# Weight sums by another engine in another half of block 6, and tails loaded at other units, in a retention and gelu kernel

**Chip, cores, metric.** One core of a Trainium2 chip. The metric is the device time of one execution in microseconds. The time is 1.6 to 1.9 us longer than the span that a trace covers.

## The reference, cut

```python
def _attn_ref(q, k, v):                     # 8 batches, 8 heads, 576 positions, 64 wide
    scores = scale * np.matmul(q, k.transpose(0, 1, 3, 2))
    Dmat = np.where(rel >= 0, gamma[:, None, None] ** rel[None, :, :], 0.0)
    return np.matmul(scores * Dmat[None], v)

def _moe_ref(x, w_in, w_out):               # x: 4608 x 512, hidden 2048
    h = x @ w_in
    g = 0.5 * h * (1.0 + np.tanh(c * (h + 0.044715 * h * h * h)))
    return g @ w_out
```

The output of the first is the input of the second. All inputs and the output are float32; the kernel computes in float16 with float32 sums.

## The kernel before

The kernel walks through nine blocks t = 0 to 8 of 512 rows: up-projection, gelu, down-projection. Between the matmuls of block t it prepares the retention of a later batch. All of it is one program with a hand-set order: `at(t, u, f)` puts f behind step ("unit") u of block t. That sets the **order on each engine's queue**, not a time. 576 = 4 x 128 + 64: the last 64 positions of a batch are its "tail", loaded by GpSimd's DMA queue, cast to float16 by GpSimd (k, q) and ScalarE (v), and turned by a DMA transpose.

The down-projection needs seven products in place of eight, of sums of the activations (`act_sums`, VectorE, in each block) and sums of the weights. Blocks 7 and 8 do the up-projection in the same way, so sums of `w_in` are needed from block 7 on (`in_sums`, the "first weights").

```python
    def in_sums(names, eng):                        # L464: 128 x 1024 float16
        for o in names:
            wu[o] = ring16().rearrange("p (k n) -> p k n", k=2)
            ...
            eng.tensor_tensor(out=wu[o], in0=x, in1=y, op=f)

    def act_sums(t, f0, f1, us=slice(0, 2), part=(0, 1)):   # four times a block, 128 x 512 float16
        ...
            nc.vector.tensor_tensor(out=s["1"], in0=a21, in1=a22, op=ALU.add)        # L588
            nc.vector.tensor_tensor(out=s["2"], in0=s["1"], in1=a11, op=ALU.subtract)  # L589
        ...
        nc.vector.tensor_tensor(out=a21, in0=a11, in1=a21, op=ALU.subtract)          # L592
        nc.vector.tensor_tensor(out=s["4"], in0=a12, in1=s["2"], op=ALU.subtract)    # L593
    ...
    TAILS = {b: ((b + 2, 5), (b + 2, 14), (b + 2, 14)) for b in range(5)}   # load; cast k, q; cast v
    TAILS |= {5: ((6, 15), (6, 24), (6, 24)), 6: ((6, 25), (7, 4), (7, 4)), 7: ((7, 5), (7, 13), (7, 13))}
    ...
    for n, o in enumerate("1324"):
        at(6, 3 + 2 * n, lambda o=o: in_sums(o, P))        # P: GpSimd
```

The product opB (L610, "m = 6") takes s2, of which the fourth group of sums writes the last part.

## Time and profile before

| | before |
|---|---|
| median of the first three runs | 302.74 us (302.4 to 303.84) |
| the execution that the profile shows | 304.62 us, span 302.8, mean clock 0.993 |
| block 6 in that profile | 35.04 us |
| blocks 3 to 5 | 30.4 to 30.5 us |

The lines of the profile stand in the prediction. There, an L number is a line of the kernel; DVE is VectorE, POOL GpSimd, ACT ScalarE, PE TensorE; a line of a timeline has start, duration, engine, line, operation, output and input, and in brackets how long the engine had been idle and whom it waited for.

### The profile page before, as it was taken

Reading aid. Unit: us, or ns where it says so; the run is one execution under the profiler, and the core shown is the slowest. Engines: PE = TensorE matmul, PEld = TensorE weight load, DVE = VectorE, ACT = ScalarE, POOL = GpSimd, SP = SyncE. Lnnn points to the kernel's source line nnn. Section 1 sums busy time; section 2 is a strip of 40 time slices with the busy share of each in tenths; the row PEclk is TensorE's granted clock in tenths of the full one; section 3 lists DMA queues with packets and bytes.
Section 4 is the critical chain, followed back from the end, with each engine's and each line's share of the span. In section 5 each row is a group of like instructions: output and inputs, shape, how many; then the busy total and the mean of one; then the engine's idle time right before and its main releaser. Section 6 shows DMA issues by size and latency. Waiting matters only on the chain.

```text
span 302.8 us, 7015 instructions
## 1 busy us (share of the span) xinstructions
PE 291.4 (96%) x2795; PEld 203.4 (67%) x2795; DVE 196.3 (65%) x387; ACT 173.4 (57%) x336; POOL 129.3 (43%) x182
## 2 busy tenths in 40 slices
PE   6999999999999999999999999999995999999994
PEld 3568755788874587458745874588454876786683
DVE  7651889578963765476448653865598457947844
ACT  6666417998666574667466746673655047513820
POOL 8678215550925079107810681069999000000000
PEclk9999999999999999999999999999999899999999
DMA  7999999999999996999699979916722032003004
GB/s 202 216 340 365 386 282 222 215 247 229 219 202 225 185 258 140 217 207 249 115 215 214 223 104 224 277 23 99 235 72 78 28 122 72 0 2 141 0 3 139
DMA packets 130433, 52.90 MB, mean 175 GB/s; under 512 B 118752, under 2 KB 121056, under 8 KB 130400
## 3 DMA queue, kind: packets, MB, share of 16 engines
q1 hardware_dynamic: 128464, 48.77, 72.9%
q0 software_dynamic: 1536, 3.15, 3.9%
q8 instruction: 22, 0.36, 0.6%
q10 hardware_dynamic: 400, 0.52, 0.5%
q14 instruction: 11, 0.09, 0.1%
HBM read 36.70 MB, written 9.44 MB: 152 GB/s over the span
## 4 chain that ended last, share of the span: by engine, by line
PE 83%; DVE 5%; SPq 4%; ACT 3%; DMA 2%; issue 1%; POOL 0%
PE hp L416 24%; PE opB L610 14%; PE opC L610 10%; PE opA L610 9%; PE hp L433 8%; PE op L550 4%; SPq L95 3%; PE st L318 3%; PE xs L368 2%; PE xs L389 2%; DMA ld<-in_moe_w_in_dram 2%; PE hB L499 2%; PE us L339 2%; DVE s L589 1%; PE hC L499 1%
## 5 line engine op out<-in xcount | busy, mean ns | idle before, releaser
L416 PE MATMUL hp<-xT,w_in_sb 128*128 128x512 f16 x384 | 88.0, 379 | 0.1
L422 ACT ACTIVATE gT<-hp 128x512 f16<-128x512 f32 x96 | 57.4, 598 | 45.7 <-PE hp L416 45.2
L416 PEld LDWEIGHTS <-w_in_sb 128*128 128x128 f16 x384 | 36.8, 98 | 41.5 <-issue 2.3
L610 PEld LDWEIGHTS <-gT 128*128 128x128 f16 x512 | 50.0, 98 | 7.3
L325 DVE TENSOR_TENSOR ret<-st,cm 128x512 f16<-128x512 f32 x64 | 40.0, 681 | 10.2 <-PE st L318 10.2
L610 PEld LDWEIGHTS <-s 128*128 128x128 f16 x384 | 37.0, 99 | 8.8 <-DVE s L589 3.4
L258 POOL TENSOR_TENSOR ck<-ld,sc 128x512 f16<-128x512 f32 x31 | 32.7, 1055 | 22.1 <-DMA ld<-in_k_dram 22.1
L588 DVE TENSOR_TENSOR s<-gT 128x512 f16<-128x512 f16 x32 | 15.8, 493 | 28.5 <-ACT gT L422 26.9
L610 PE MATMUL opA<-w_out_sb,gT 128*128 128x256 f16 x256 | 30.6, 273 | 0.0
L610 PE MATMUL opB<-wt,gT 128*128 128x256 f16 x256 | 30.4, 273 | 0.0
L433 PE MATMUL hp<-xT,w_in_sb 128*128 128x256 f16 x256 | 29.8, 273 | 0.5 <-POOL w_in_sb L685 0.4
L861 POOL COPY gate<-s 128x1 f16<-128x1 f16 x5 | 0.9, 189 | 62.7 <-DVE s L593 62.7
L433 PEld LDWEIGHTS <-w_in_sb 128*128 128x128 f16 x256 | 24.6, 98 | 3.9 <-POOL w_in_sb L685 0.7
L258 POOL TENSOR_TENSOR cq<-ld,sc 128x512 f16<-128x512 f32 x24 | 25.8, 1076 | 2.0 <-DMA ld<-in_q_dram 1.8
L662 ACT COPY ost<-opA 128x512 f32<-128x512 f32 x8 | 4.7, 586 | 31.9 <-PE opA L610 28.6
L439 ACT ACTIVATE gT<-hp 128x512 f16<-128x512 f32 x32 | 19.0, 600 | 5.9 <-PE hp L433 5.8
L406 ACT CAST xT<-xs 128x512 f16<-128x512 f32 x32 | 18.4, 585 | 3.1 <-PE xs L389 2.7
L625 DVE TENSOR_TENSOR ost<-k,opC 128x512 f32<-128x512 f32 x15 | 10.3, 687 | 15.2 <-PE opC L610 14.9
L360 ACT CAST tbd<-ws 64x256 f16<-64x256 f32 x48 | 19.3, 403 | 1.4 <-DVE ws L355 0.8
L625 DVE TENSOR_TENSOR k<-k,opB 128x512 f32<-128x512 f32 (+1 forms) x18 | 11.2, 627 | 12.1 <-PE opB L610 10.6
L610 PE MATMUL opB<-wt,s 128*128 128x256 f16 x128 | 15.5, 273 | 3.1 <-DVE s L589 3.1
L589 DVE TENSOR_TENSOR s<-s,gT 128x512 f16<-128x512 f16 x32 | 16.1, 504 | 1.1
(126 smaller groups left out, 437.9 us busy)
## 6 DMA issues: line engine op xcount, KB each, us to landing
ld<-in_q_dram SPq DMA_DIRECT2D x32, 256.0 KB, 5.1
ld<-in_k_dram SPq DMA_DIRECT2D x32, 256.0 KB, 5.2
ld<-in_v_dram SPq DMA_DIRECT2D x32, 256.0 KB, 5.0
out_dram<-ost SPq DMA_DIRECT2D x16, 512.0 KB, 5.2
ld<-in_moe_w_in_dram SPq DMA_DIRECT2D x16, 256.0 KB, 5.5
ld<-in_moe_w_out_dram SPq DMA_DIRECT2D x16, 256.0 KB, 5.7
lt<-in_k_dram POOLq DMA_DIRECT2D x16, 64.0 KB, 4.5
lt<-in_q_dram POOLq DMA_DIRECT2D x16, 64.0 KB, 4.1
```

The costliest lines, as they stand in the source:

```text
L258: eng.tensor_tensor(out=dst.rearrange("p (h d) -> p h d", d=D), in0=raw.rearrange("p (h d) -> p h d", d=D), in1=sc[:, s0 : s0 + nh].unsque ...
L325: nc.vector.tensor_tensor(out=r, in0=st[hl][:, 0:w], in1=m.rearrange("p n i -> p (n i)"), op=ALU.mult)
L360: cp(out=(tbd[b % 2][r, c, :, r] if c < NC - 1 else tbt[b % 4][r, :, r]), in_=att[b]["w", c][r])
L406: nc.scalar.copy(out=xT[:, g0 : g0 + 2], in_=src)
L416: nc.tensor.matmul(hp.rearrange("p (g t) -> p g t", t=TL), w_in_sb[:, ct, 128 * fc : 128 * fc + 128], xT[:, o : o + TB // TL, ct, :], star ...
L422: nc.scalar.activation(out=gT[t][:, fc].rearrange("p i n -> p (i n)"), in_=hp, func=AF.Gelu_apprx_tanh)
L433: nc.tensor.matmul(hp[:, 256 * x : 256 * x + 256].rearrange("p (g t) -> p g t", t=TL), w_in_sb[:, ct, 128 * (f + x) : 128 * (f + x) + 128] ...
L439: nc.scalar.activation(out=gT[t][:, f : f + 2, 2 * u : 2 * u + 2, :].rearrange("p f i n -> p f (i n)"), in_=hp.rearrange("p (f n) -> p f n ...
L588: nc.vector.tensor_tensor(out=s["1"], in0=a21, in1=a22, op=ALU.add)
L589: nc.vector.tensor_tensor(out=s["2"], in0=s["1"], in1=a11, op=ALU.subtract)
L610: nc.tensor.matmul(op[tag, u][:, HD * u : HD * u + HD], lhs(f), rhs[:, f], start=(new and (u == 0 or own) and f == 0), stop=(f == NH - 1), ...
L625: nc.vector.tensor_tensor(out=o, in0=a, in1=b, op=ALU.add)
```

## The change

Intent: take the weight sums of w_in from GpSimd, where they run beside VectorE's activation sums, and give them to VectorE in the second half of block 6, where it has idle spells of 2.54 and 3.21 us in the trace of before. The tails of batches 4 to 7 are set to other units, so that their casts fit the new order.

```diff
     TAILS[0] = ((2, 5), (2, 20), (2, 20))
-    TAILS |= {5: ((6, 15), (6, 24), (6, 24)), 6: ((6, 25), (7, 4), (7, 4)), 7: ((7, 5), (7, 13), (7, 13))}
+    TAILS |= {4: ((6, 2), (6, 12), (6, 12)), 5: ((6, 18), (6, 26), (6, 26))}
+    TAILS |= {6: ((6, 27), (7, 5), (7, 5)), 7: ((7, 6), (7, 13), (7, 13))}
@@
     for n, o in enumerate("1324"):
-        at(6, 3 + 2 * n, lambda o=o: in_sums(o, P))
+        at(6, (22, 24, 26, 28)[n], lambda o=o: in_sums(o, V))
```

## The prediction

> **What bounds the kernel now.** I read the page first: which engine is busy, and which chain ended last.
>
> ```profile
> PE 291.4 (96%) x2795; PEld 203.4 (67%) x2795; DVE 196.3 (65%) x387; ACT 173.4 (57%) x336; POOL 129.3 (43%) x182
> ...
> PEclk9999999999999999999999999999999899999999
> ...
> PE 83%; DVE 5%; SPq 4%; ACT 3%; DMA 2%; issue 1%; POOL 0%
> ```
>
> TensorE (PE) is busy 96% of the span and carries 83% of the chain. Two things stand out: 5% of the chain lies on VectorE (DVE), and one slice of forty, near 235 us, has a lower clock. So I took the busy times of each engine by block. A block starts where the first up-projection matmul (L416) follows the last opB product of the block before: 89.3, 119.5, 149.9, 180.3, 210.8 for blocks 2 to 6, and 245.8 for block 7.
>
> ```profile
> core 0: us, PE busy (x) PEld busy (x) DVE busy (x) ACT busy (x) POOL busy (x), PEclk, DMA share, GB/s
> ...
> 149.90:180.30 30.40, 30.38 (x297) 20.25 (x296) 17.88 (x38) 18.42 (x36) 12.93 (x18) 1.00 0.97 184
> 180.30:210.80 30.50, 30.48 (x298) 20.24 (x296) 17.87 (x38) 18.42 (x36) 13.05 (x15) 1.00 0.83 165
> 210.80:245.80 35.00, 31.87 (x282) 20.80 (x281) 23.55 (x35) 15.59 (x30) 24.21 (x32) 0.95 0.34 93
> ```
>
> Blocks 3 to 5 take 30.4 to 30.5 us with PE never idle. Block 6 takes 35.0 us, though it has 16 matmuls fewer (no state products for a further block). GpSimd (POOL) is busy 24.2 us there instead of 13, and VectorE 23.6 instead of 17.9 with three instructions fewer: they take longer each. The loss sits in that block alone. Where it falls, the timelines of VectorE and GpSimd over the first half of block 6 say:
>
> ```profile
> 215.14 0.84 DVE L588 TENSOR_TENSOR s<-gT 128x512 f16<-128x512 f16 x1 [3.62 <-ACT gT L422]
> 216.01 2.22 DVE L589 TENSOR_TENSOR s<-s,gT 128x512 f16<-128x512 f16 x1
> 218.16 2.34 DVE L592 TENSOR_TENSOR gT<-gT 128x512 f16<-128x512 f16 x1
> 220.42 0.83 DVE L593 TENSOR_TENSOR s<-gT,s 128x512 f16<-128x512 f16 x1
> 221.17 2.47 DVE L325 TENSOR_TENSOR ret<-st,cm 128x512 f16<-128x512 f32 x4
> ...
> 230.57 1.40 DVE L588 TENSOR_TENSOR s<-gT 128x512 f16<-128x512 f16 x1
> 232.01 0.42 DVE L589 TENSOR_TENSOR s<-s,gT 128x512 f16<-128x512 f16 x1
> ```
> ```profile
> 213.55 2.14 POOL L464 TENSOR_TENSOR ld<-w_in_sb 128x1024 f16<-128x1024 f16 x1
> 215.77 2.19 POOL L464 TENSOR_TENSOR ld<-ld,w_in_sb 128x1024 f16<-128x1024 f16 x1
> 218.03 2.19 POOL L464 TENSOR_TENSOR ld<-w_in_sb,ld 128x1024 f16<-128x1024 f16 x1
> ```
>
> In block 5 the same four activation sums (L588 to L593) take 0.42 us each (184.69 to 186.2). Here two take 2.22 and 2.34, each ending within 0.3 us of the GpSimd weight sum (L464) beside it. L325, which reads one operand from PSUM, keeps its 0.62 each.
>
> ```profile
> 228.56 0.82 PE L610 MATMUL opB<-wt,s 128*128 128x256 f16 x6
> 232.49 1.29 PE L610 MATMUL opB<-wt,s 128*128 128x256 f16 x10 [3.11 <-DVE s L589]
> ...
> 234.68 3.04 PE L610 MATMUL opC<-wt,s 128*128 128x256 f16 x16
> ```
>
> PE gets six products into opB and waits 3.11 us for the last sum s2. Afterwards opC's sixteen products take 3.04 us instead of 1.9; the stretches 232.5 to 234.7 and 234.7 to 237.7 show a granted clock of 0.75 and 0.62. The loss is thus 3.11 us of waiting plus the slow clock behind it.
>
> [...] 2.22 against 0.42 us for the sums, no change for L325. [...] Here a gap of 3.11 us is followed by 0.62 to 0.75 for about 5 us. [...] The eight weight sums of w_out (L576), of the same 128x1024 f16 size as L464[...]: 0.68 us where nothing disturbs them, against 2.2 us on GpSimd.
>
> **The change, part by part.**
> (1) *Removed from GpSimd:* four L464, 2.31 + 2.14 + 2.19 + 2.19 = 8.8 us, of which the last three meet VectorE's sums. VectorE's excess against 0.42 each is 0.42 + 1.80 + 1.92 + 0.41 = 4.55 us up to 221.2; the last 0.41 belongs to the cast of tail 4, which begins at 220.18. Later casts of tails 5 and 6 (at 225.4 and 230.4) add 0.86 + 0.41 + 0.43 + 0.98 = 2.7 us. Together 7.2 us. Block 5 has slack for 1.59 + 2.11 = 3.7 us (its idle times before L325 and before the fourth L588). 7.2 − 3.7 = 3.5, close to the 3.11 us for which PE waited and the 0.3 us by which block 5's last s2 comes early. This closes, so the cause is settled for me.
> (2) *Added to VectorE:* four L464 at 0.68 us, 2.7 us, at units 22 to 28 of block 6, between the additions of products m7, m3 and m4. VectorE has idle spells of 2.54 and 3.21 us there now. In the order of the built program each weight sum stands ahead of an addition that waits for PE anyway; only the last one has less than 1 us of room: it follows the m3 addition (done about 0.7 us after opC) and must end before opB is done, 1.75 us after opC. 0.69 + 0.68 = 1.37 us fit. Cost on the path: 0, at worst 0.2.
> (3) *Moved: tails.* With L464 gone, tail 4's loads start at 207.6 (six issues of 0.62), as tail 3's did at 177.13, so its casts run at 211.3 to 214.3, ahead of VectorE's first sums at 215.1. Tail 5's loads follow (3.7 us), its casts fall between 216.3 and 219.3: at worst they touch the last of the first four sums, where 1.59 us is free. Tail 6's v load waits for ScalarE's cast of tail 4's v, now behind the thirteenth gelu (223.05 + 0.6 + 0.4 = 224.1); add 1.2 us of issue: casts at 225.3 to 226.6, beside the state sums at 224.3 to 226.1, at most 0.8 us lost out of the 2.11 free. The fourth L588 to L593 (228.2 in block 5's rhythm) then run undisturbed.
> (4) *The end of block 6:* tail 5's transposes now follow both output stores, so tail 7's casts come some 5 us after the start of block 7 instead of 3.2. Its transposes then land about 12 us after it; PE needs them 19.3 us after it (scores at 265.14 now). No cost.
>
> Sum: block 6 goes from 35.04 (210.79 to 245.83) to block 5's 30.45 less the state products, 0.27 by PE's timeline: 30.18. Gain 4.86 us (3.11 wait, about 1.75 clock). 302.74 − 4.86 = 297.9; with 0.1 for small collisions, **298.0 us**, 1.6% faster.
>
> **The rivals.**
> *A. A cast of tail 6 meets the fourth group of sums.* If the v load of tail 6 comes 2 us later than I think, its two casts (1.2 us) block L588/L589 at 228 as at 230.57 before (1.40 us), and PE waits about 1 us. For it: the margin rests on one ScalarE cast; against it: that cast moves forward by two units. [...] It would give 299.
> *B. The new sums delay VectorE's additions or the x sums at the block's end.* The first 7-product step of block 7 needs both (hB starts at 247.40, 1.57 us after the block's start, just after L480's second at 247.34). If a store's wait or a late cast pushes a weight sum, each 0.5 us shows one to one: 298.5 to 299.5. For: there is no room between L480 and hB now. Against: the sums stand before the additions that bound L480 already.
> *C. The clock drop is not the wait's doing.* Then only 3.11 + 0.27 come back: 299.4. Against it: no other block shows a drop, and it begins exactly behind the gap.
> *D. Nothing is gained, as another wait takes over* (block 7's transposes, or the score of tail 4 at unit 17). The 7 us margin in (4) speaks against it; it would give 301 to 303.
>
> **Range and chances.** The mechanism closes in numbers, and what stands above 298.0 are A, B and C, each costing about 1 us and each less than one in six. Below 297.4 nothing is left to gain, as PE is then busy throughout. Range 297.3 to 299.6. A gain over 2% needs 296.7, which no part of the sum supplies: 3%. Slower by 2% would need a new stall of 11 us: 1%.
>
> **What would show it right or wrong.** Right: block 6 lasts 30.1 to 30.4 us at clock 1.00; the wait of opB for L589 is gone; all sixteen activation sums of that block take about 0.42 us with at most three longer ones; L464 on VectorE takes 0.7 us; blocks 2 to 5 and 7 keep their lengths within 0.2. Wrong: a wait of opB for s2 above 0.5 us (A), hB of block 7 waiting for an L464 or L480 (B), a clock under 0.9 in block 6 without a wait (C), or a score of block 7 waiting for a transpose (D).

## The result and the profile after

The changed kernel takes **299.76 us** (median; 299.74 to 300.2, four runs), beside 303.29 us for the kernel before over its then four runs (302.4 to 304.56). The ratio is 0.9884 (95% interval 0.9843 to 0.9925): a gain clear of the noise, but within 2%. Ratios here are the mean time of one kernel's fast runs over that of the other's of the same rounds, so not quite the ratio of the medians quoted. 299.76 lies above the range of the prediction (297.3 to 299.6).

The page of the changed kernel, the same lines as were shown of before:

```profile
PE 288.9 (97%) x2795; PEld 202.0 (68%) x2795; DVE 191.7 (64%) x391; ACT 173.3 (58%) x336; POOL 120.2 (40%) x178
...
PEclk9999999999999999999999999999999999999999
...
PE 89%; SPq 4%; ACT 3%; DMA 2%; issue 0%; POOL 0%; DVE 0%
```

VectorE has left the chain (5% before), and the slice of lower clock is gone. The busy times by block, of blocks 5 and 6:

```profile
core 0: us, PE busy (x) PEld busy (x) DVE busy (x) ACT busy (x) POOL busy (x), PEclk, DMA share, GB/s
180.50:210.90 30.40, 30.38 (x297) 20.20 (x296) 17.87 (x38) 18.42 (x36) 12.97 (x18) 1.00 0.87 164
210.90:241.10 30.20, 30.18 (x283) 20.03 (x281) 19.98 (x39) 15.46 (x30) 14.98 (x25) 1.00 0.45 109
```

Block 6 (210.93 to 241.12 by the chain) takes 30.19 us, with TensorE busy throughout at full clock. VectorE's timeline in block 6:

```profile
215.27 0.43 DVE L588 TENSOR_TENSOR s<-gT 128x512 f16<-128x512 f16 x1 [3.62 <-ACT gT L422]
215.73 0.42 DVE L589 TENSOR_TENSOR s<-s,gT 128x512 f16<-128x512 f16 x1
216.07 0.42 DVE L592 TENSOR_TENSOR gT<-gT 128x512 f16<-128x512 f16 x1
...
225.99 1.23 DVE L355 TENSOR_TENSOR ws<-vs,gt 128x256 f32<-128x256 f32 x1
...
236.12 0.68 DVE L464 TENSOR_TENSOR ld<-w_in_sb 128x1024 f16<-128x1024 f16 x1
```

The sums that took 2.22 and 2.34 us take 0.42 now; a weight sum costs VectorE 0.68. One state sum (L355) still takes 1.23 us in place of 0.42, beside tail 6's casts (225.73 to 226.9), but nothing waits for it. And TensorE runs opB in one piece, without the wait of 3.11 us:

```profile
228.70 1.91 PE L610 MATMUL opB<-wt,s 128*128 128x256 f16 x16
```

So the mechanism came out as forecast, block 6 even to 0.01 us. The span fell from 302.8 to 298.1, by 4.7 us. Yet the times fell by 3.0 to 3.5. So the *comparison* has to be looked at: is the execution that was traced like the others?

### The profile page after: what moved, and what is told of

It is laid out like the page before. It is cut to its first block, busy times and chain, and to the rows that moved or that the text cites.

```text
span 298.1 us, 7015 instructions
## 1 busy us (share of the span) xinstructions
PE 288.9 (97%) x2795; PEld 202.0 (68%) x2795; DVE 191.7 (64%) x391; ACT 173.3 (58%) x336; POOL 120.2 (40%) x178
## 3 DMA queue, kind: packets, MB, share of 16 engines
q0 software_dynamic: 1536, 3.15, 4.3%
## 4 chain that ended last, share of the span: by engine, by line
PE 89%; SPq 4%; ACT 3%; DMA 2%; issue 0%; POOL 0%; DVE 0%
PE hp L416 28%; PE opB L610 14%; PE opC L610 10%; PE opA L610 9%; PE hp L433 8%; PE op L550 4%; SPq L95 3%; PE st L318 3%; PE xs L368 3%; DMA ld<-in_moe_w_in_dram 2%; PE xs L389 2%; PE hB L499 2%; PE us L339 2%; PE hC L499 1%; PE hA L499 1%; PE tr L288 1%
## 5 line engine op out<-in xcount | busy, mean ns | idle before, releaser
L325 DVE TENSOR_TENSOR ret<-st,cm 128x512 f16<-128x512 f32 x64 | 40.0, 682 | 11.7 <-PE st L318 11.7
L588 DVE TENSOR_TENSOR s<-gT 128x512 f16<-128x512 f16 x32 | 14.6, 457 | 29.2 <-ACT gT L422 27.6
L433 PE MATMUL hp<-xT,w_in_sb 128*128 128x256 f16 x256 | 29.8, 273 | 1.1 <-POOL w_in_sb L685 1.0
L433 PEld LDWEIGHTS <-w_in_sb 128*128 128x128 f16 x256 | 24.6, 98 | 4.4 <-POOL w_in_sb L685 1.2
L685 DVE CAST w_out_sb<-ld 128x512 f16<-128x512 f32 x16 | 8.9, 579 | 12.0 <-DMA ld<-in_moe_w_out_dram 11.8
L245 ACT CAST cv<-ld 128x512 f16<-128x512 f32 x27 | 16.3, 619 | 0.3
```

The costliest lines, as they stand in the source:

```text
L245: eng.copy(out=dst, in_=raw)
L325: nc.vector.tensor_tensor(out=r, in0=st[hl][:, 0:w], in1=m.rearrange("p n i -> p (n i)"), op=ALU.mult)
L433: nc.tensor.matmul(hp[:, 256 * x : 256 * x + 256].rearrange("p (g t) -> p g t", t=TL), w_in_sb[:, ct, 128 * (f + x) : 128 * (f + x) + 128] ...
```

## The experiments

**T1**: every execution of before loses the wait of 3.1 us, but the clock drop behind it comes in some only. **T2**: the wait itself differs between executions. **T3**: the spread comes from another part of the program. Beside these stands the question which part of the change does the work, and why. All outputs are right.

### Is the profiled execution a typical one?

before_again is the kernel before, unchanged, five rounds.

> The kernel before, unchanged, for its spread and the clock of each execution. T1 (the wait of about 3 us is there in every execution, the clock drop behind it only in some): times spread from 302.4 to 304.6 us, and the mean clock falls with the time, from 0.998 or more in the fastest to 0.993 in the slowest; a traced execution with a time near 302.5 shows a wait of about 3 us and a clock near 1.00 behind it. T2 (the length of the wait differs): the clock is the same in all executions, and the wait of a fast one is some 1 to 2 us shorter than 3.11. T3 (the spread comes from elsewhere): block 6 lasts 35.0 us in all traces, and another block or the start differs.

Its six runs: 301.57 to 304.47 us. Two at a clock of 0.991 and 0.992 took 304.47 and 304.3; four at 0.998 or more took 301.57 to 303.1. Over all calls, 55 executions of the kernel before were timed beside the others: 21 with a mean clock of 0.994 or less at 303.69 to 305.37 us (mean 304.5), 34 with 0.996 or more at 301.49 to 303.52 (mean 302.1); all together 303.0. The second group alone is 2 us wide. The traces below have a slow stretch of clock in every execution at 0.993 or less and in none at 0.997 or more, so I take the 21 for the executions with a drop. The profiled execution of 304.62 is one of this group, and of its slower half.

after_again is the changed kernel, unchanged, with three more traces of before.

> The changed kernel, unchanged, on one chip with the kernel before. If before loses a wait in every execution and the clock drop only in some: the changed kernel 299.7 to 300.2 with a clock of 0.996 or more in every execution and no time above 300.5, the kernel before in two groups (about 301.6 to 303.1 at 0.997 or more, about 304.4 at 0.994 or less).

299.65 to 300.32 us, clock 0.996 to 0.999: within 0.12 us of what was expected. Ratio 0.9897 (0.9851 to 0.9943). Ten runs of the changed kernel have a mean of 300.0.

Five looks at the kernel before, for their traces:

> One more trace of the kernel before. T1: the wait of opB for s2 is 2.9 to 3.2 us whatever the time, and the clock behind it decides between 302.5 to 303.1 and 304.4. T2: in an execution near 301.6 to 302.5 the wait is 1.8 to 2.6 us, as a VectorE sum and a GpSimd instruction met in another order, and no slow clock follows.

> As before_b: one more trace. T1: wait 2.9 to 3.2 us in any case. T2: a shorter wait where the time is shorter.

> As before_b: one more trace. T1: wait 2.9 to 3.2 us in any case. T2: a shorter wait where the time is shorter.

> One more trace of the kernel before. If its time is 301.5 to 302.1: a wait of 1.6 to 2.2 us and no slow clock behind it. If 303.0 to 303.3: a wait of about 3 us and no slow clock. If 304 or more: slow clock.

> As before_e: one more trace. If its time is 301.5 to 302.1: a wait of 1.6 to 2.2 us and no slow clock. If 303.0 to 303.3: about 3 us and no slow clock. If 304 or more: slow clock.

The table puts all seven traces of before in order. "Rest" is block 6 less 30.19 us (the changed kernel's) less the wait. The last column is a mean over 9 us.

| execution | time us | wait of opB for s2 | block 6 | rest | clock from 229 to 238 us |
|---|---|---|---|---|---|
| before | 304.62 | 3.11 | 35.04 | 1.74 | 0.81 |
| before_again | 304.47 | 2.98 | 34.88 | 1.71 | 0.81 |
| before_c | 303.89 | 2.36 | 34.30 | 1.75 | 0.81 |
| before_b | 303.78 | 2.36 | 34.35 | 1.80 | 0.81 |
| before_f | 302.3 | 1.98 | 32.35 | 0.18 | 1.00 |
| before_e | 301.57 | 1.11 | 31.49 | 0.19 | 1.00 |
| before_d | 300.73 | 1.11 | 31.47 | 0.17 | 1.00 |

T2 holds: one and the same program waits 1.11 to 3.11 us. (before_e was expected to wait 1.6 to 2.2 us at its time and waited 1.11.) T1 holds in part: the clock drop comes with some waits only. A wait without it has a rest of 0.17 to 0.19 us all the same, so of the 1.71 to 1.80 us the drop itself costs some 1.5 to 1.6. T3 has a small share: before_d and before_e have the same block 6 and differ by 0.84 us, as block 6 starts at 210.58 in one and 211.38 in the other; the two are already 0.86 us apart at L433, 20.75 and 21.61 us into the program. How the wait differs, the timelines of before_d show: TensorE's wait, VectorE at the fourth group of sums, GpSimd at the casts:

```profile
230.28 1.26 PE L610 MATMUL opB<-wt,s 128*128 128x256 f16 x10 [1.11 <-DVE s L589]
```
```profile
229.34 0.42 DVE L588 TENSOR_TENSOR s<-gT 128x512 f16<-128x512 f16 x1
229.79 0.42 DVE L589 TENSOR_TENSOR s<-s,gT 128x512 f16<-128x512 f16 x1
230.14 0.83 DVE L592 TENSOR_TENSOR gT<-gT 128x512 f16<-128x512 f16 x1
```
```profile
225.67 0.66 POOL L258 TENSOR_TENSOR ek<-lt,sc 128x256 f16<-128x256 f32 x1 [0.56 <-DMA lt<-in_q_dram]
...
230.73 0.71 POOL L258 TENSOR_TENSOR ek<-lt,sc 128x256 f16<-128x256 f32 x1
```

The four sums beside L464 are as slow here as in the first trace (0.81, 2.23, 2.34, 0.83 us, from 214.92). The difference comes later. Tail 5's cast waited 0.56 us for its load, and the second group of sums slipped past it (in the first trace L592 took 1.28 there; here the third group lost 0.7 us to the casts instead). The fourth group was ahead of tail 6's cast, where in the first trace the cast began 0.17 us before L588 and held it up to 1.40. In before_e, with the same wait of 1.11 us, L588 and L589 of the fourth group also took 0.42 each; in the other five traces at least one of the two took 0.83 or more. So which engine is first at these points sets the wait, and nothing in the program orders them. Why a load comes later in one execution than in another is not shown.

before_fill keeps the loss, but leaves TensorE no idle time: 14 matmuls on zeros in the place of the wait.

```diff
+    at(6, 17, lambda: filler(14, "hp"))
```

> The kernel before with 14 idle-filling matmuls (14 x 0.216 = 3.0 us of work into a free bank) in the place where TensorE waited for s2 in block 6. T1: TensorE never idles there, so its clock stays at 1.00 in all executions; block 6 takes 33.3 to 33.6 us, times 302.6 to 303.2 with a spread under 0.5 us, no faster than the fast executions of before and faster than its slow ones. T2: the spread of before stays (302.4 to 304.6).

302.7 to 303.26 us, the clock at 0.997 or more in all six runs, block 6 33.22 us (33.3 to 33.6 expected); a spread of 0.56 in place of 3 us. TensorE's timeline:

```profile
228.97 3.19 PE L217 MATMUL fill<-wide,ident 128*128 128x512 f16 x14
231.99 1.91 PE L610 MATMUL opB<-wt,s 128*128 128x256 f16 x16
```

Without that idleness none of the six runs shows the slow clock (0.997 or more), though 3 us are still lost (33.22 us against 30.19). Ratio to before 1.0014 (0.9982 to 1.0046): on average the filler costs about what it saves.

### What length of wait brings the slow clock?

Here the changed kernel gets a wait made on purpose. First with dummy additions on VectorE ahead of the fourth group of sums (into a tile that is dead by then):

```diff
+    at(6, 15, lambda: [V.tensor_tensor(out=wide, in0=cm..., in1=cm..., op=ALU.add) for _ in range(7)])   # 5, 4
```

> The changed kernel with seven dummy additions on VectorE (7 x 0.62 us, into a dead tile) ahead of the fourth group of sums in block 6, so that s2 comes some 3.1 us late and nothing else of before is there. If an idle TensorE alone brings the clock drop, in some executions and not in others: a wait of opB of 2.6 to 3.3 us in the trace; times in two groups, 302.6 to 303.3 at a clock of 0.997 or more and 304.3 to 305.0 at 0.994 or less. If the drop needs something else of the kernel before: all executions 302.6 to 303.3 at 0.997 or more.

> after_gap with five dummy additions. They took 0.87 us each there, not 0.62, and seven made a wait of 4.33 us, so five make 4.33 - 2 x 0.87 = 2.6 us. If the drop is a matter of chance at such a wait: most executions at 302.5 to 303.0 with a clock of 0.997 or more, some at 303.8 to 305.0 with 0.994 or less. If the length alone decides: all in one group.

> after_gap with four dummy additions: a wait of 4.33 - 3 x 0.87 = 1.7 us. No drop in any execution, 301.6 to 302.1, clock 0.996 or more, as tails_only had none at 2.1 us. If a drop comes here too, its condition isn't the length of the wait.

after_gap: 305.09 to 307.65 us, clock 0.986 to 0.994 in all six, a wait of 4.33 us in the trace, not 3.1. after_gap5: three runs at 302.78 to 302.86 (clock 0.997 to 1.0), three at 304.58 to 305.1 (0.991 to 0.993), and the trace has 3.15, not 2.6. after_gap4: five runs at 301.8 to 303.27 without the drop and, against expectation, one at 303.99 with it (0.991); 1.60 us in the trace, which is of the run at 301.8. These three are **confounded**: an addition takes 0.69 us alone, but up to 1.56 us beside tail 6's casts (the trace of after_gap5), so the made wait can differ from run to run, as that of before does. My "0.87 each" was such a mean, and wrong. That is why two more kernels make the wait on ScalarE, with copies ahead of the last gelu:

```diff
+    at(6, 14, lambda: [A.copy(out=wide, in_=cm...) for _ in range(6)])   # 8
```

> The changed kernel with six dummy copies on ScalarE (0.475 us from start to start) ahead of block 6's last gelu, so that the fourth group of sums comes 2.85 us late; less 0.55 us of room, a wait of opB of 2.3 us in every execution. If the drop is a matter of chance at this wait: two groups, 302.4 to 302.8 at a clock of 0.997 or more and 304.1 to 304.6 at 0.994 or less. If the length alone decides: one group.

> As act_gap6 with eight copies: a wait of 3.2 us in every execution. If the drop is a matter of chance: 303.3 to 303.7 at 0.997 or more and 305.0 to 305.5 at 0.994 or less, with more in the second group than for act_gap6. If the length alone decides: all at 305.0 to 305.5.

The copies took 0.65 us each, so the waits came out longer than planned: 3.08 and 4.38 us in the traces. act_gap6: 304.62 to 305.93 us, clock 0.991 to 0.994 in **all six** runs. act_gap8: 305.8 to 307.59, 0.988 to 0.992 in all six. No second group. TensorE in act_gap6, then its clock by stretches (the figure behind the busy times):

```profile
232.80 1.72 PE L610 MATMUL opB<-wt,s 128*128 128x256 f16 x10 [3.08 <-DVE s L589]
...
235.42 2.61 PE L610 MATMUL opC<-wt,s 128*128 128x256 f16 x16
```
```profile
233.00:235.00 2.00, 2.00 (x22) 1.41 (x22) 0.78 (x3) 1.54 (x5) 0.00 (x0) 0.61 0.00 0
235.00:237.00 2.00, 2.00 (x19) 1.36 (x16) 2.00 (x4) 0.00 (x0) 0.00 (x0) 0.53 0.04 8
237.00:239.00 2.00, 2.00 (x21) 1.80 (x19) 1.31 (x3) 0.00 (x0) 0.00 (x0) 1.00 0.00 0
```

So idleness of TensorE (3.08 us in this trace) brings the drop here (0.61 and 0.53 in the two stretches), with no GpSimd weight sum in play. With act_gap6's six copies it came in six of six executions; the one traced waited 3.08 us, and the times of the six spread over 1.3 us, so the wait may not be the same in all. At 2.36 us it came in both traced executions, at 2.09 us (tails_only, below) or less in none of those traced. Chance alone, as T1 had it, is unlikely after six of six, but the length of the wait doesn't settle it either: executions without a drop at 303.01 to 303.52 us (before) and 303.27 us (after_gap4) must have waited for some 2.5 to 3.0 us (an estimate: these times less the slowest changed run, 300.32, less 0.17), longer than 2.36. No trace of one was caught.

The same traces, cut into finer stretches (in the first one the drop lies from 233.59 to 237.01 us), add this. In all nine traces with a drop (between 228 and 246 us) the clock is 0.50 for 3.41 us (for twice that in after_gap and sums_p_late, with waits of 4.33 and 5.59 us) and 1.00 before and after. The drop begins between 2.0 us before TensorE resumes (after_gap) and 1.3 us after that (before_b), and in the 3.41 us just before it TensorE was idle for 2.1 to 3.4 us. So in these traces the slow clock lasts 3.41 us or twice that, and its start is not tied to that of the wait. Why one execution with a wait of some 3 us drops and another doesn't is not shown. As an estimate, 3.41 us at 0.50 in place of 1.00 would cost 1.7 us; in the four traces of before with a drop, block 6 lost a little less to it, 1.5 to 1.6 us (the rest of 1.71 to 1.80 less the 0.17 to 0.19 us of a wait without a drop).

### Which part of the change does it?

sums_only moves the weight sums and leaves the tails; tails_only does the reverse.

> Only the weight sums moved to VectorE, tails as before. The GpSimd order is then the same as in the changed kernel; the cast of tail 4's v on ScalarE stands two units later, so tail 6's v load and casts come some 3 us later and meet the fourth group of sums at 228. If the moved tails matter: a wait of opB for s2 of 0.3 to 1 us, 300.0 to 300.8. If they don't: 299.7 to 299.9, as the changed kernel.

> Only the tails moved, the weight sums stay on GpSimd in the first half. If the sums beside VectorE's activation sums are the cause: two of the four L464 still meet them, block 6 stays at 32 to 35 us, 301.5 to 304 us. If the tails alone were the cause: 299.8.

sums_only: 300.28 to 301.03 us, ratio 0.9934 (0.9902 to 0.9966). tails_only: 301.86 to 302.98, ratio 0.9993 (0.996 to 1.0026), a wait of 2.09 us and no drop in six runs. The weight sums are the matter. But sums_only stays some 0.5 us behind the changed kernel (medians 300.57 against 300.14 and 299.76), and the one traced execution shows a cause, in VectorE, GpSimd and TensorE:

```profile
228.24 0.73 DVE L588 TENSOR_TENSOR s<-gT 128x512 f16<-128x512 f16 x1 [1.62 <-ACT gT L422]
229.01 0.72 DVE L589 TENSOR_TENSOR s<-s,gT 128x512 f16<-128x512 f16 x1
```
```profile
227.51 1.22 POOL L83 DMA_DIRECT2D lt<-in_v_dram  x2 [1.95 <-ACT ev L245]
228.75 0.69 POOL L258 TENSOR_TENSOR ek<-lt,sc 128x256 f16<-128x256 f32 x1
```
```profile
229.78 1.27 PE L610 MATMUL opB<-wt,s 128*128 128x256 f16 x10 [0.36 <-DVE s L589]
```

GpSimd's queue waited 1.95 us for ScalarE's cast of tail 4's v, so tail 6's casts met the fourth group of sums: the collision that the moved tails avoid (in the changed kernel the same load waits 0.26 us and the casts are over at 226.9).

sums_v_early keeps the old place and takes the new engine; sums_p_late the reverse.

```diff
# sums_v_early, from before              # sums_p_late, from after
-   at(6, 3 + 2 * n, ... in_sums(o, P))   -   at(6, (22, 24, 26, 28)[n], ... in_sums(o, V))
+   at(6, 3 + 2 * n, ... in_sums(o, V))   +   at(6, (22, 24, 26, 28)[n], ... in_sums(o, P))
```

> The weight sums on VectorE at their old units 3, 5, 7, 9, tails as before: the engine without the place. If the engine matters: two of the four fall into VectorE's idle times (211.7 and 216.8), two delay the second and third group of sums by 1.4 us, which the slack of 2.1 us takes but for the casts; wait 0.3 to 1.5 us, 300.3 to 301.5. If the place in the first half were the matter: as before, 302 to 304.

> The weight sums on GpSimd at the new units 22 to 28, tails moved: the place without the engine. GpSimd's queue has nothing that holds it back, so the first two run right after tail 5's loads, at 218 to 222.7, and meet the second group of sums (221.5), the others the third and fourth. If the engine matters: a wait of opB of 1 to 3 us, 301 to 303.5. If moving them later in the program were enough: 299.7 to 300.3.

sums_v_early: 300.55 to 300.91 us, a wait of 0.36 us, ratio 0.9919 (0.9873 to 0.9965), as sums_only. sums_p_late: 307.65 to 310.23 us, some 2% *slower* than before (ratio 1.0191, 1.0139 to 1.0244: clear of the noise, but unclear whether by 2%), a wait of 5.59 us, beyond my range. On VectorE the unit in the program hardly matters; on GpSimd the later unit is worse than the old one (tails_only, with the same tails, waits 2.09 us). A later unit is not a much later time there: nothing holds GpSimd's queue back, and it runs the "late" sums as soon as its loads are issued, beside the second and third group. A GpSimd run of the sums that really falls into the second half was not tried. VectorE and GpSimd in sums_p_late:

```profile
221.51 1.68 DVE L588 TENSOR_TENSOR s<-gT 128x512 f16<-128x512 f16 x1
223.23 0.72 DVE L589 TENSOR_TENSOR s<-s,gT 128x512 f16<-128x512 f16 x1
223.87 2.91 DVE L592 TENSOR_TENSOR gT<-gT 128x512 f16<-128x512 f16 x1
```
```profile
218.68 4.22 POOL L464 TENSOR_TENSOR ld<-w_in_sb 128x1024 f16<-128x1024 f16 x2
```

### What in a GpSimd instruction blocks VectorE?

p_memset is sums_only with four memsets (128x512) in the old place of each of the four sums: GpSimd is as busy, but reads nothing.

```diff
+    for n in range(4):
+        at(6, 3 + 2 * n, lambda: [P.memset(wide, 0.0) for _ in range(4)])
```

> As sums_only (weight sums late on VectorE, tails as before), with four GpSimd memsets of 0.54 us each in the place of each of the four L464 on GpSimd. The same GpSimd time, but nothing read from SBUF. If only a GpSimd instruction that reads SBUF blocks VectorE's two-input instructions: the first four sums keep 0.42 us, the wait of opB stays at 0 to 0.6 us, 300.2 to 301.1. If any GpSimd instruction blocks them: sums of 2 us, times as before (301.6 to 304.5).

300.01 to 301.03 us, ratio 0.9899 (0.9849 to 0.995), no wait in the trace. VectorE, then GpSimd:

```profile
216.37 0.42 DVE L588 TENSOR_TENSOR s<-gT 128x512 f16<-128x512 f16 x1 [3.62 <-ACT gT L422]
216.82 0.42 DVE L589 TENSOR_TENSOR s<-s,gT 128x512 f16<-128x512 f16 x1
```
```profile
214.76 6.95 POOL L848 MEMSET wide<- 128x512 f16 x12
```

Twelve memsets lie over the whole first group, and each sum keeps 0.42 us. The wait says less here, as the memsets also put tail 6's casts off to 231.59, behind the fourth group; so with the tails unmoved the kernel is about as fast as the changed one (median 300.2). So it is not GpSimd's being busy that slows these sums: 0.42 us beside memsets, 2.22 us beside L464 in before. The memsets read nothing and L464 reads SBUF; that the reading makes the difference is my conclusion from this pair, which also differs in the length of one instruction (0.58 against some 2.2 us).

## Why the prediction was wrong

- **What bounds block 6** (TensorE waits for s2, as L464 on GpSimd blocks VectorE's sums): right. p_memset and sums_p_late show it from both sides (sums of 0.42 us beside memsets and no wait; sums of up to 2.91 us with L464 and casts on GpSimd, and a wait of 5.59).
- **The clock drop belongs to the wait** (rival C rejected): right as to the cause; act_gap6 makes it by idleness of TensorE without a GpSimd weight sum. But the prediction booked it as a fixed 1.75 us. Its size was right (1.71 to 1.80, of which 0.17 to 0.19 comes with a wait alone), its presence was not: 21 of 55 executions. "0.62 to 0.75 for about 5 us" were means over stretches cut too wide: it is 0.50 for 3.41 us, from 233.6. And rival C's sum counts 0.27 us too much: block 6 lacks these state products before the change as well, so C gives 302.74 − 3.11 = 299.6.
- **(1) and (2), the costs on VectorE**: right, 0.68 us each for the weight sums, none on the path.
- **(3) the tails**: nearly right. Tail 4's casts came at 213.4 to 214.7 (forecast 211.3 to 214.3), still ahead of the sums. Tail 5's casts came at 219.9 and 221.2, not 216.3 to 219.3, the second of them after a wait for its load; tail 6's at 225.7 to 226.9 (forecast 225.3 to 226.6), with the loss of 0.8 us on a state sum that was allowed for. Rival A, put at under one in six, did not come; sums_only shows it without the moved tails, at 0.36 us of wait in place of 1 and with the clock at 1.00 from 229 to 238 us. B and D did not come either: in the changed trace TensorE waits for nothing from 180 us on.
- **(4) the end of the block**: right, tail 7's casts at 245.40, 4.3 us into block 7 (forecast some 5).
- **Sum**: block 6 at 30.19 (forecast 30.18), a gain of 4.85 us *against the traced execution*. Then "302.74 − 4.86 = 297.9". **This subtraction is the step that failed.** The 4.86 us were read from an execution that took 304.62 us, the 302.74 is the median of three others. 304.62 − 4.86 = 299.76, which is what was measured; that it fits to the last digit is luck, as time less wait less rest gives 299.45 to 300.27 for the seven traces. Nor would the right base have been enough, since the gain of 4.86 us is that of one execution. The mean loss over the executions of before is 303.0 − 300.0 = 3.0 us, against the forecast 4.86: the wait is not 3.11 us as a rule but 1.11 to 3.11 in seven traces, and the clock drop comes in 21 of 55. As an estimate from these, 1.55 x 21 / 55 = 0.6 us is the drop's share and some 2.4 us are the wait and what comes with it; the seven traces have a mean wait of 2.14 us, plus 0.18.
- **"This closes, so the cause is settled for me"**: the closed sum (7.2 − 3.7 = 3.5 against 3.11) was true of the trace, and the experiments bear the cause out; but it said nothing on whether the trace is typical. None of the rivals asked that. The hint was in the numbers: three runs of a program on one core that spread over 1.4 us, and a profiled one above them all.

## What to carry to other kernels

Take the loss that a trace shows from the time of the traced execution, never from a median of others; where the runs spread more than those of a kernel without the stall (3 to 4 us here, 0.7 after the change), the stall itself varies, and one trace shows one draw. A collision between two queues that nothing orders is such a draw: here the wait differed by 2 us between executions, and the idle time then cost up to 1.6 us more by way of the clock. Look at what VectorE runs beside a GpSimd instruction that reads SBUF: here its sums with two inputs in SBUF took 2.22 and 2.34 us beside L464 in place of 0.42, while L325, with one input in PSUM, kept its 0.62 beside two L464 (sums_p_late, 218.45 to 220.9). And a later place in the program is not a later time: there the "late" sums on GpSimd began at 218.68 us, in the first half of block 6.
